# Feed-forward products of two float16 parts in place of two float32r parts, in a kernel of recurrent attention and a max-out feed-forward

## The chip, the cores and the metric

The kernel runs on one core of a Trainium2 chip. The metric is the device time of one launch in microseconds (us), the lower the better. A core has a matrix engine (TensorE: PE for its matmuls, PEld for its weight loads), a vector engine (VectorE, DVE), a scalar engine (ScalarE, ACT), GpSimd (POOL), and SyncE (SP), which here only issues DMAs. Each engine has its own list of instructions; they wait for one another through semaphores.

## The reference

```
for t in range(S):                                   # attention: B=4, H=8, S=768, D=48
    cur = einsum('bhd,bhe->bhde', u * k[t], v[t])
    y[t] = einsum('bhd,bhde->bhe', r[t], state + cur)
    state = w * state + einsum('bhd,bhe->bhde', k[t], v[t])
x = y reshaped to (3072 tokens, 384)
h = maximum(maximum(x @ w1, x @ w2), x @ w3)         # w1, w2, w3: 384 x 768
out = h @ w_out                                      # w_out: 768 x 384
```

The feed-forward weights arrive as 64-bit floats, everything else as float32.

## The kernel before

**Stages.** The 768 steps are cut into 12 chunks of 64. Within a chunk the recurrence is written as matmuls: `scores` (24 per half of the heads, r against k), `keys` (24, k against v, which gives the new state) and `values` (48, which gives the attention output), for each of two halves q of the heads. These matmuls read float16 pairs: each number is a high part plus a low part, and a product is three matmuls (high by high, high by low, low by high; `three`, L407). Their weights are 128x128 and 64 or 48 columns move through. The block-shaped weights (`kb`, `ktb`, `vb`, `sb`) are spread from dense tiles by DMAs that SP issues (`spread`, L318); each is a single buffer.

**Feed-forward.** Of each chunk (256 tokens) `x_high` and `x_low` (L463, L467) take the attention output from PSUM into two parts, xh on ACT and xl on DVE. For each of six blocks f of 128 hidden columns and each of the three weights i, `up` (L498) makes nine matmuls of 128x128 by 256 columns into one PSUM bank: three blocks j of the inner dimension, times three products of parts. `first` (ACT, L505) copies the result of i = 0 to m, `least` (DVE, L510) takes the maximum with i = 1 and 2, `h_high` (ACT) and `h_low` (DVE, or POOL for f below 5 from chunk 1 on) split m into parts hh and hl. `down` (L532) makes 54 matmuls a chunk for the output, `leaving` (ACT) copies them out, and ACT issues their DMAs. So a chunk has 162 + 54 = 216 feed-forward matmuls, 2592 in all. All of their operands are of type float32r (F32R): a float32 whose high part keeps 12 bits, and a low part. A matmul of this type is one instruction of the program, which loads its weights itself. PSUM has four banks for these results (`psm`), each used again when DVE or ACT has read it.

**Weights.** In the first 75 us the eight weight tiles, each as two halves, are loaded and turned from 64-bit floats into parts: `tops` (ACT), `convert` (DVE), `round_up` (ACT, the high part), `leave` (DVE, the low part). The conversion holds for ordinary numbers only, so at the end the kernel loads all weights again (`again`, L706: a DMA of 576 KB, `vet_words` on DVE and `vet_sum` on ACT for each half) and counts exponents out of bounds. `check` (DVE, L562) joins this with sums of squares of r, k, v and the state (`square_sum`, ACT), a matmul of one column (`count`) adds up over partitions, and `verdict` sets a flag. Where the flag is set, `general` (L584) computes everything anew; it does not run with these inputs.

**Order.** Each piece of work is noted by `do` (L65) with an engine, a due time in chunks, a cost and what it reads and writes. `Plan.order` (L84) plays them through as a list scheduler: at each step it takes the ready piece that can start first, and among those close together the one with the earliest due time, shifted by kind through a table (`SHIFT`, L46). The order of the play is the program's order on each engine. A changed cost or an added piece can thus move any piece behind it. For chunks up to 2 DVE does the work that POOL does later (`helper`, L360).

Of the kernel before, what the change touches and what calls it, by code (L numbers as in the profile page):

```python
# [26 lines left out]
U = 8  # L27
# [7 lines left out]
SC_X = 2.0 ** -23  # L35
# [115 lines left out]
def kernel(ctx, tc, feat, tok, wu, ut, ws, wo, cst, out):  # L151
# [102 lines left out]
    beyond = const.tile([P, 1], F32, name="beyond")  # L254
    nc.gpsimd.memset(beyond, -14.5 * 2 ** 23)

    def uppers(raw):
        return raw.bitcast(I32)[:, 0:2 * HN].rearrange("p (n two) -> p n two", two=2)[:, :, 1]

    def vet_words(raw):  # L260
        t = uppers(raw)
        nc.vector.tensor_scalar(out=t, in0=t, scalar1=0x3F800000, scalar2=0x7F800000, op0=ALU.bitwise_xor, op1=ALU.bitwise_and)

    def vet_sum(k, raw):
        t = uppers(raw)
# [78 lines left out]
    stat = const.tile([P, 4, 2 * NCH], F32, name="stat")  # L344
    nc.vector.memset(stat[:, 3], 0.0)

    def square_sum(src, kind, c, q, scale=1.0):
        junk = tmp.tile([P, U, D], BF16, name="junk", bufs=1)
        nc.scalar.activation(out=junk, in_=src, func=AF.Square, scale=scale, accum_out=stat[:, kind, 2 * c + q:2 * c + q + 1])  # L349
# [117 lines left out]
    def x_low(c, q, xh, xl):  # L467
        ps = raws[c, q].pop("va")
        for (hi, src), (lo, _) in zip(x_parts(xh, q, ps), x_parts(xl, q, ps)):
            nc.vector.scalar_tensor_tensor(out=lo, in0=src, scalar=SC_X, in1=hi.bitcast(F32), op0=ALU.mult, op1=ALU.subtract)  # L470

# [25 lines left out]

    def up(x, f, i, n):  # L498
        ps = psm.tile([P, n], F32, name="psm")
        prods = [(wup[:, f, i, j, :], t[:, j, :]) for j in range(NJ) for t in x]  # L500
        prods += [(by_up(lows[f], i, j), x[0][:, j, :]) for j in range(NJ)]
        pairs3(ps, prods)
        return ps

    def first(ps, n):  # L505
        m = tmp.tile([P, n], F32, name="m", bufs=3)
        nc.scalar.copy(out=m, in_=ps)  # L507
        return m

    def least(ps, m, to):  # L510
        nc.vector.tensor_tensor(out=to, in0=ps, in1=m, op=ALU.max)  # L511
# [7 lines left out]
    def h_low(c, h, f, m):  # L519
        lows_by(c, f).tensor_tensor(out=h[1][:, f, :], in0=m, in1=h[0][:, f, :].bitcast(F32), op=ALU.subtract)  # L520

    def up_all(x, h, f, n):
        for i in range(3):
            ps = up(x, f, i, n)
            if i == 0:
                m = first(ps, n)
            else:
                least(ps, m, m)
        h_high(h, f, m)
        h_low(0, h, f, m)  # L530
# [31 lines left out]
    def check():  # L562
        ok = small.tile([P, 8 * NCH + 1 + 2 * NF + 4], F32, name="ok")
# [5 lines left out]
        nc.vector.tensor_scalar(out=ok[:, 8 * NCH + 1:], in0=odd, scalar1=0.0, scalar2=None, op0=ALU.is_equal)  # L569
        got["good"] = small.tile([P, 1], F32, name="good")  # L570
        nc.vector.tensor_reduce(out=got["good"], in_=ok, axis=AX.X, op=ALU.min)
# [12 lines left out]
    def general():  # L584
        def convert_any(n, h):
            hi, lo = part_of(n, h)
# [16 lines left out]
            nc.vector.tensor_tensor(out=t, in0=t, in1=m, op=ALU.bitwise_or)  # L603
            t = t.bitcast(F32)
            nc.scalar.copy(out=hi, in_=t)
            nc.vector.tensor_tensor(out=lo, in0=t, in1=hi.bitcast(F32), op=ALU.subtract)
# [38 lines left out]
        with tc.For_i(0, NCH // 2, 1) as i:  # L645
            for b in range(B):
# [14 lines left out]
                x = xtile(P)  # L661
                nc.scalar.copy(out=x[0], in_=ps)
                nc.vector.tensor_tensor(out=x[1], in0=ps, in1=x[0].bitcast(F32), op=ALU.subtract)
                h = [hp.tile([P, NF, P], F32R, name=f"h{s}") for s in "hl"]
                for f in range(NF):
                    up_all(x, h, f, P)
# [145 lines left out]
    def leave_x(c, q, due):  # L812
        def x_hi():
            if q == 0:
                T["x", c] = [xp.tile([P, NJ, TOK], F32R, name="xh"), None]
            x_high(c, q, T["x", c][0])

        def x_lo():
            if q == 0:
                T["x", c][1] = xp.tile([P, NJ, TOK], F32R, name="xl")  # L820
# [23 lines left out]
    def ffn(c):  # L844
        x = [("xh", c), ("xl", c)]
        for f in range(NF):
            due = c + 0.11 * f
            for i in range(3):
# [3 lines left out]
                do(due + 0.035 * i, "pe", 1.075, mul, reads=[*x, *["stirred"] * (not c and not f), *((a, f, h) for a in ("his", "lo") for h in parts[i])], takes=[("psm", ("up", c, f, i))])  # L852
                if i == 0:
                    do(due - 0.2, "act", act(TOK), lambda f=f: do_tile(("m", c, f), first(T["up", c, f, 0], TOK)), reads=[("up", c, f, 0)], writes=[] if f else [("begun", c)], takes=[("m", ("m", c, f))])
                    continue
                do(due + 0.035 * i - 0.2, "dve", dve(TOK), lambda f=f, i=i: least(T["up", c, f, i], T["m", c, f], T["m", c, f]), reads=[("up", c, f, i)], writes=[("m", c, f)])

            def hi(f=f):
                if f == 0:
                    T["h", c] = [hp.tile([P, NF, TOK], F32R, name="hh")]  # L860
                h_high(T["h", c], f, T["m", c, f])

            def lo(f=f):
# [49 lines left out]
    do(NCH - 0.4, "dve", 1.5, check, reads=["ends", "odd", *(k for k in plan.wrote if k[0] == "sq")], writes=["good"])  # L913
# [67 lines left out]
```

## Time and profile before

| | |
|---|---|
| three runs | 417.0, 418.95 and 419.32 us, median 418.95 |
| the profiled execution | span of 415.5 us from first to last instruction; its launch is not timed apart, and the runs are 1.5 to 3.8 us longer than this span |
| PE, PEld | 394.2 us (95%), 388.5 us (94%), 4768 matmuls |
| DVE | 284.0 us (68%) |
| ACT | 257.7 us (62%) |
| POOL | 183.5 us (44%) |
| DMA | 90.13 MB, mean 217 GB/s |

Matmuls are pipelined: one of 256 columns is recorded as some 285 ns long though the next starts about 118 ns after it. What a matmul costs is therefore read from the distance between starts, or from a stretch of many divided by their count.

### The profile page before, as it was taken

What the parts mean: (1) busy time and instruction counts of PE and PEld (TensorE: products, weight loads), DVE (VectorE), ACT (ScalarE), POOL (GpSimd) and SP (SyncE); (2) the same over time, 40 slices, a digit from 0 to 9 for tenths busy, and PEclk for the clock granted to TensorE, in tenths of its full rate; (3) what the DMA queues carried; (4) which work ended last, traced back from release to release, by engine and by line L of the source; (5) the groups of instructions that cost most, each with busy time, mean ns of one, the idle gap of its engine ahead of it and who ended that gap; (6) DMA issues with size and microseconds to landing.
All of it is one profiled execution on the core that took longest, in us unless ns stands there. A gap on an engine that the chain in (4) does not pass through costs nothing.

```text
span 415.5 us, 11992 instructions
## 1 busy us (share of the span) xinstructions
PE 394.2 (95%) x4768; PEld 388.5 (94%) x4768; DVE 284.0 (68%) x551; ACT 257.7 (62%) x674; POOL 183.5 (44%) x181
## 2 busy tenths in 40 slices
PE   2889899989999999999999999999999999999995
PEld 2768899989999999999999999999999999999994
DVE  6888999988697676767566567566667596353340
ACT  5999987885766556465456466465465476365331
POOL 9000000287668663764664764764664560020120
PEclk9996999999999999999999999999999999999999
DMA  7898998889899887795785785785785996886001
GB/s 280 319 321 210 268 298 273 230 230 265 210 280 243 241 225 189 224 238 142 227 222 152 231 235 144 227 228 150 229 231 130 321 290 147 262 288 206 24 3 44
DMA packets 30959, 90.13 MB, mean 217 GB/s; under 512 B 4784, under 2 KB 9648, under 8 KB 30896
## 3 DMA queue, kind: packets, MB, share of 16 engines
q1 hardware_dynamic: 25568, 84.47, 71.2%
q10 hardware_dynamic: 5328, 4.82, 3.7%
q8 instruction: 39, 0.64, 0.7%
q14 instruction: 24, 0.20, 0.2%
HBM read 45.85 MB, written 4.72 MB: 122 GB/s over the span
## 4 chain that ended last, share of the span: by engine, by line
PE 72%; ACT 9%; DMA 7%; DVE 7%; issue 2%; POOL 1%; SPq 0%; ACTq 0%; DVEq 0%; POOLq 0%
PE psm L496 61%; PE psa L409 11%; ACT junk L349 2%; DMA ktb<-ktd 2%; DMA kb<-kd 2%; ACT ztop L239 2%; DMA out_dram<-io 1%; DVE m L511 1%; DVE wl L250 1%; ACT xh L465 1%; ACT wh L246 1%; DMA sb<-sd 1%; DVE feat L366 1%; ACT kb L476 1%; DVE kd L337 1%
## 5 line engine op out<-in xcount | busy, mean ns | idle before, releaser
L496 PE MATMUL psm<-xh,wh 128*128 128x256 f32 x648 | 165.8, 286 | 2.1 <-ACT m L507 1.3
L496 PE MATMUL psm<-xl,wh 128*128 128x256 f32 x648 | 163.1, 282 | 1.3 <-DVE xl L470 1.3
L496 PEld LDWEIGHTS psm<-xh,wh 128*128 128x128 f32 x648 | 122.9, 190 | 3.0 <-ACT m L507 1.5
L496 PEld LDWEIGHTS psm<-xl,wh 128*128 128x128 f32 x648 | 122.5, 189 | 1.8 <-DVE xl L470 1.8
L496 PE MATMUL psm<-xh,wl 128*128 128x256 f32 x648 | 112.5, 283 | 0.0
L511 DVE TENSOR_TENSOR m<-psm,m 128x256 f32<-128x256 f32 x144 | 60.4, 420 | 67.4 <-PE psm L496 59.3
L496 PEld LDWEIGHTS psm<-xh,wl 128*128 128x128 f32 x648 | 92.6, 189 | 0.0
L366 POOL TENSOR_TENSOR feat<-feat,wrt 128x512 f32<-128x512 f32 x36 | 47.5, 1332 | 76.8 <-DVE sd L339 69.1
L520 POOL TENSOR_TENSOR hl<-m,hh 128x256 fp32r<-128x256 f32 x55 | 45.8, 835 | 68.6 <-ACT hh L514 68.6
L514 ACT CAST hh<-m 128x256 fp32r<-128x256 f32 x72 | 28.9, 405 | 58.0 <-DVE m L511 57.6
L496 PE MATMUL psm<-hh,woh 128*128 128x256 f32 x216 | 54.3, 284 | 0.0
L496 PE MATMUL psm<-hh,wl 128*128 128x256 f32 x216 | 53.4, 279 | 0.0
L385 POOL TENSOR_TENSOR am<-tok,u_sb 128x384 f32<-128x384 f32 x18 | 20.7, 1151 | 61.3 <-DVE al L429 61.3
L349 ACT ACTIVATE junk<-tok 128x384 bf16<-128x384 f32 x72 | 37.4, 520 | 9.2 <-DMA tok<-in_tok_dram 7.6
L496 PEld LDWEIGHTS psm<-hh,woh 128*128 128x128 f32 x216 | 40.6, 188 | 0.0
L496 PEld LDWEIGHTS psm<-hh,wl 128*128 128x128 f32 x216 | 40.6, 188 | 0.0
L470 DVE SCALAR_TENSOR_TENSOR xl<-psa,xh 32x256 fp32r<-32x256 f32 (+2 forms) x60 | 28.3, 472 | 14.1 <-ACT xh L465 13.2
L465 ACT ACTIVATE xh<-psa 32x256 fp32r<-32x256 f32 (+2 forms) x60 | 25.1, 418 | 17.1 <-PE psa L409 16.2
L496 PE MATMUL psm<-hl,woh 128*128 128x256 f32 x216 | 35.1, 280 | 0.0
L409 PE MATMUL psa<-ah,vb 128*128 128x64 f16 x352 | 32.8, 194 | 1.4 <-ACT junk L349 1.4
L507 ACT COPY m<-psm 128x256 f32<-128x256 f32 x72 | 26.4, 368 | 10.0 <-PE psm L496 8.7
L409 PE MATMUL psa<-rh,sb 128*128 128x64 f16 x352 | 32.5, 193 | 0.0
(102 smaller groups left out, 741.4 us busy)
## 6 DMA issues: line engine op xcount, KB each, us to landing
tok<-in_tok_dram SPq DMA_DIRECT2D x24, 576.0 KB, 6.6
raw<-in_ws_dram SPq DMA_DIRECT2D x24, 576.0 KB, 7.7
feat<-in_feat_dram SPq DMA_DIRECT2D x24, 512.0 KB, 5.4
kb<-kd SPq DMA_DIRECT2D x22, 256.0 KB, 5.1
kb<-kd SPq DMA_DIRECT2D x22, 248.0 KB, 5.6
ktb<-ktd SPq DMA_DIRECT2D x20, 256.0 KB, 3.5
ktb<-ktd SPq DMA_DIRECT2D x20, 248.0 KB, 4.1
raw<-in_wo_dram SPq DMA_DIRECT2D x8, 576.0 KB, 5.6
```

Source lines behind the costliest of these rows:

```text
L239: nc.scalar.copy(out=ztop[h].bitcast(F16).rearrange("p (n two) -> p n two", two=2)[:, :, 1], in_=halves(raw[:, 1:], 3).bitcast(BF16))
L349: nc.scalar.activation(out=junk, in_=src, func=AF.Square, scale=scale, accum_out=stat[:, kind, 2 * c + q:2 * c + q + 1])
L366: helper(c).tensor_tensor(out=t[n], in0=t[n], in1=tb, op=ALU.mult)
L385: helper(c).tensor_tensor(out=w.rearrange("p (g b) d -> p g b d", g=2), in0=t["r"], in1=by_token(u_sb, q), op=ALU.mult)
L409: nc.tensor.matmul(out=ps, lhsT=l[i], rhs=rr[j], start=first and n == 0, stop=last and n == 2)
L465: nc.scalar.mul(out=hi, in_=src, mul=SC_X)
L470: nc.vector.scalar_tensor_tensor(out=lo, in0=src, scalar=SC_X, in1=hi.bitcast(F32), op0=ALU.mult, op1=ALU.subtract)
L496: nc.tensor.matmul(out=ps, lhsT=a, rhs=b, start=first and n == 0, stop=last and n == len(prods) - 1)
L507: nc.scalar.copy(out=m, in_=ps)
L511: nc.vector.tensor_tensor(out=to, in0=ps, in1=m, op=ALU.max)
L514: nc.scalar.copy(out=h[0][:, f, :], in_=m)
L520: lows_by(c, f).tensor_tensor(out=h[1][:, f, :], in0=m, in1=h[0][:, f, :].bitcast(F32), op=ALU.subtract)
```

## The change

All feed-forward operands become pairs of float16 in place of pairs of float32r: weights (one tile per weight block that holds both parts, `wsp`), xh and xl, hh and hl. Powers of two keep them in the range of the type (`X16`, `W16`, `H16`), so copies out of PSUM become multiplications: `first` and `leaving` on ACT, and `least` on DVE, which becomes a scalar_tensor_tensor in place of a tensor_tensor. `leave`, too, becomes a scalar_tensor_tensor. A float16 matmul of the program is two instructions, a weight load and a matmul.

The second load of the weights goes, with `vet_words` and `vet_sum`; in place of them ACT squares and sums the high part of each half weight (`weight_sum`, 16 times 576 columns) and of each chunk's x (`x_sum`, 12 times 768 columns), and `check` compares those sums with bounds: 17 instructions in place of 12. The planner's costs of `up` and `down` are lowered. `general` computes in plain float32.

```diff
-SC_X = 2.0 ** -23
+X16, W16, H16 = 2.0 ** 13, 2.0 ** 14, 2.0 ** -20
+SC_X = X16 * 2.0 ** -23
+SC_O = 1.0 / (X16 * W16 * W16 * H16)
...
-    wup = const.tile([P, NF, 3, NJ, P], F32R, name="wh")
-    wdn = const.tile([P, NF, DM], F32R, name="woh")
-    odd = const.tile([P, 2 * NF + 4], F32, name="odd")
+    wsp = [const.tile([P, 2, WN], F16, name=f"w{n}") for n in range(NW)]
+    wsq = const.tile([P, 2 * NW], F32, name="wsq")
...
-    lows = [const.tile([P, WN], F32R, name=f"wl{n}") for n in range(NW)]
...
     def round_up(n, h, raw):
-        nc.scalar.copy(out=part_of(n, h)[0], in_=mids(raw).bitcast(F32))
+        nc.scalar.mul(out=part_of(n, h)[0], in_=mids(raw).bitcast(F32), mul=W16)
 
     def leave(n, h, raw):
         hi, lo = part_of(n, h)
-        nc.vector.tensor_tensor(out=lo, in0=mids(raw).bitcast(F32), in1=hi.bitcast(F32), op=ALU.subtract)
...
+        nc.vector.scalar_tensor_tensor(out=lo, in0=mids(raw).bitcast(F32), scalar=W16, in1=hi, op0=ALU.mult, op1=ALU.subtract)
+
+    def squared(src, to):
+        junk = tmp.tile([P, NJ * TOK], BF16, name="junk", bufs=1)
+        nc.scalar.activation(out=junk[:, 0:src.shape[1]], in_=src, func=AF.Square, accum_out=to)
+
+    def weight_sum(n, h):
+        squared(part_of(n, h)[0], wsq[:, 2 * n + h:2 * n + h + 1])
...
+    def x_sum(c, xh):
+        squared(xh.rearrange("p j n -> p (j n)"), xsq[:, c:c + 1])
...
-    def first(ps, n):
+    def first(ps, n, by):
         m = tmp.tile([P, n], F32, name="m", bufs=3)
-        nc.scalar.copy(out=m, in_=ps)
+        nc.scalar.mul(out=m, in_=ps, mul=by)
         return m
 
-    def least(ps, m, to):
-        nc.vector.tensor_tensor(out=to, in0=ps, in1=m, op=ALU.max)
+    def least(ps, m, by):
+        nc.vector.scalar_tensor_tensor(out=m, in0=ps, scalar=by, in1=m, op0=ALU.mult, op1=ALU.max)
...
     def again(n, h, due):
-        w = ("vet", n, h)
-
-        def fetch():
-            T[w] = load_weight(n, h)
-
-        dma(due, fetch, 8 * P * HN, reads=[("begun", int(due))], takes=[("raw64", w)])
-        do(due + 0.4, "dve", 0.4, lambda: vet_words(T[w]), writes=[w])
-        do(due + 0.5, "act", act(HN) + 0.1, lambda: vet_sum(2 * n + h, T[w]), reads=[w], writes=["odd"])
+        do(due + 0.5, "act", act(HN) + 0.1, lambda: weight_sum(n, h), reads=[("his", n, h), ("begun", int(due))], writes=[("wsq", n, h)])
...
+        if q:
+            do(due + 0.9, "act", act(NJ * TOK) + 0.1, lambda: x_sum(c, T["x", c][0]), reads=[hi], writes=[("xsq", c)])
...
-                do(due + 0.035 * i, "pe", 1.075, mul, reads=[*x, *["stirred"] * (not c and not f), *((a, f, h) for a in ("his", "lo") for h in parts[i])], takes=[("psm", ("up", c, f, i))])
+                do(due + 0.035 * i, "pe", 0.983, mul, reads=[*x, *["stirred"] * (not c and not f), *((a, f, h) for a in ("his", "lo") for h in parts[i])], takes=[("psm", ("up", c, f, i))])
...
-            do(due, "pe", len(fs) * 0.358, lambda: down(T["h", c], m, fs, banks, TOK), reads=reads, **(dict(takes=[("psm", bank)]) if 0 in fs else dict(writes=[bank])))
+            do(due, "pe", len(fs) * 0.328, lambda: down(T["h", c], m, fs, banks, TOK), reads=reads, **(dict(takes=[("psm", bank)]) if 0 in fs else dict(writes=[bank])))
```

From chunk 4 on PE keeps its order of stages: in both programs a chunk's round is 99 `up` matmuls, values, keys and scores, 54 `down` matmuls, 45 `up`, values, 9 `up`, keys, 9 `up`, scores. Earlier the order shifts. Three places matter for what follows.

**PE, from chunk 2 to chunk 3.** In the program before, PE's last rows ahead of chunk 3's first `up` (operands xh and xl, weights wh) are the `down` of chunk 2 (hh and hl); values, scores and keys stand ahead of those 54:

```order
L496 MATMUL psm<-hh,woh 128x256
L496 MATMUL psm<-hh,wl_108 128x256
L496 MATMUL psm<-hh,woh 128x256
L496 MATMUL psm<-hh,wl_108 128x256
L496 MATMUL psm<-hl,woh 128x256 x6
L496 MATMUL psm<-xh,wh 128x256
L496 MATMUL psm<-xl,wh 128x256
```

In the changed program (weights w_98 to w_105) the last `down` rows of chunk 2 stand ahead of the 48 values matmuls (vb, sb), which make the second half of chunk 3's x:

```order
L487 LDWEIGHTS w_105
L487 MATMUL psm<-hl,w_105 128x256
L487 LDWEIGHTS w_105
L487 MATMUL psm<-hl,w_105 128x256
L400 LDWEIGHTS vb_135
L400 MATMUL psa<-ah,vb_135 128x64
```

Behind these 48 come 24 scores and 24 keys matmuls (ktb), and then at once chunk 3's first `up`:

```order
L400 LDWEIGHTS ktb
L400 MATMUL psa<-vd_143,ktb 128x48
L400 LDWEIGHTS ktb
L400 MATMUL psa<-vd_143,ktb 128x48
L487 LDWEIGHTS w_98
L487 MATMUL psm<-xh,w_98 128x256
L487 LDWEIGHTS w_98
L487 MATMUL psm<-xl,w_98 128x256
```

So between the values matmuls and the `up` that reads their result stand 48 matmuls of 64 or 48 columns now, and stood 102 before, 54 of them of 256 columns.

**ACT, at chunk 0's x.** Before, behind the last rows of `x_high` (L465), the first evacuation of an `up` (L507, m from psm) stands behind the work on r, the diagonal (am), the squares and three `round_up` (wh):

```order
L465 ACTIVATE xh<-psa 32x256 x3
L239 CAST ztop_110<-raw_275 128x576
L246 CAST wh<-raw_268 128x576
L371 CAST rh<-feat 128x512
L476 ACTIVATE ktb<-tok 64x8x48 x2
L397 ACTIVATE am<-cs,a 128x64 x8
L239 CAST ztop_109<-raw_295 128x576
L349 ACTIVATE junk,stat<-tok 128x384 x3
```

In the changed program the sum of squares of x (xsq) is put in, and the first evacuation (L502) is the eighth row behind `x_high`:

```order
L456 ACTIVATE xh<-psa 32x256 x3
L237 CAST ztop_108<-raw_272 128x576
L244 ACTIVATE w_100<-raw_265 128x576
L252 ACTIVATE junk,xsq<-xh 128x768
L362 CAST rh<-feat 128x512
L467 ACTIVATE ktb<-tok 64x8x48 x2
L237 CAST ztop_107<-raw_292 128x576
L244 ACTIVATE w_100<-raw_272 128x576
L502 ACTIVATE m<-psm 128x256
```

Before, that evacuation was the row behind the fourth `round_up` that follows `x_high`; two of these `round_up`, the diagonal, the squares and the parts of v, state and k now stand behind it.

**The last chunk.** On ACT of the changed program the last three sums over weights (wsq) stand behind the first evacuation of chunk 11:

```order
L502 ACTIVATE m<-psm 128x256
L252 ACTIVATE junk,wsq<-w_104 128x576
L252 ACTIVATE junk,wsq<-w_105 128x576 x2
L509 CAST hh<-m 128x256
L502 ACTIVATE m<-psm 128x256
```

On DVE `check` reads them (its last rows here), two `least` rows into chunk 11, and ends in the row that writes good:

```order
L541 TENSOR_TENSOR ok<-ok,bt 128x12
L539 TENSOR_SCALAR bt<-wsq 128x16
L540 TENSOR_SCALAR ok<-wsq 128x16
L541 TENSOR_TENSOR ok<-ok,bt 128x16
L559 TENSOR_REDUCE good<-ok 128x1
L506 SCALAR_TENSOR_TENSOR m<-psm,m 128x256 x2
L567 TENSOR_SCALAR flag<-psa 1x1
```

PE's `count`, which reads good, stood behind 126 of chunk 11's 162 `up` matmuls and stands behind 54 of them now.

More of the change, by code (lines that the diff above doesn't have):

```diff
@@ L200, with part_of, exact @@
     NW = NF + 2
+    wsp = [const.tile([P, 2, WN], F16, name=f"w{n}") for n in range(NW)]
+    wsq = const.tile([P, 2 * NW], F32, name="wsq")
+    def part_of(n, h):
+        return [wsp[n][:, s, h * HN:(h + 1) * HN] for s in range(2)]
+    def exact(n):
+        return wsp[n].rearrange("p s n -> p (s n)").bitcast(F32)
     def by_up(t, i, j):
@@ L344 @@
     stat = const.tile([P, 4, 2 * NCH], F32, name="stat")
+    xsq = const.tile([P, NCH], F32, name="xsq")
     nc.vector.memset(stat[:, 3], 0.0)
     def square_sum(src, kind, c, q, scale=1.0):
-        junk = tmp.tile([P, U, D], BF16, name="junk", bufs=1)
-        nc.scalar.activation(out=junk, in_=src, func=AF.Square, scale=scale, accum_out=stat[:, kind, 2 * c + q:2 * c + q + 1])
+        junk = tmp.tile([P, NJ * TOK], BF16, name="junk", bufs=1)
+        nc.scalar.activation(out=junk[:, 0:U * D].rearrange("p (u d) -> p u d", u=U), in_=src, func=AF.Square, scale=scale, accum_out=stat[:, kind, 2 * c + q:2 * c + q + 1])
     def units(a):
@@ L519, in h_low @@
     def h_low(c, h, f, m):
[L520 to L530, printed above, removed]
+        lows_by(c, f).tensor_tensor(out=h[1][:, f, :], in0=m, in1=h[0][:, f, :], op=ALU.subtract)
     def down(h, m, fs, banks, n):
@@ L536, in down, with w, leaving @@
         ms = slice(m * P, (m + 1) * P)
-        prods = [(t, hh[:, f, :]) for f in fs for t in (wdn[:, f, ms], by_down(lows[NF + f // 3], f, ms))]
-        prods += [(wdn[:, f, ms], hl[:, f, :]) for f in fs]
+        def w(f, s):
+            return by_down(wsp[NF + f // 3][:, s], f, ms)
+        prods = [(w(f, s), hh[:, f, :]) for f in fs for s in range(2)]
+        prods += [(w(f, 0), hl[:, f, :]) for f in fs]
         pairs3(banks[m], prods, 0 in fs, NF - 1 in fs)
-    def leaving(ps, n):
+    def leaving(ps, n, by):
         o = tmp.tile([P, n], F32, name="io", bufs=3)
-        nc.scalar.copy(out=o, in_=ps)
+        nc.scalar.mul(out=o, in_=ps, mul=by)
         return o
-    def xtile(n):
-        return [xp.tile([P, NJ, n], F32R, name=f"x{s}") for s in "hl"]
     def bounded(dst, src, lo, hi):
@@ L602, in convert_any @@
             ts(out=m, in0=rw[:, :, 1], scalar1=-2 ** 31, scalar2=None, op0=ALU.bitwise_and)
[L603 to L606, printed above, removed]
+            nc.vector.tensor_tensor(out=exact(n)[:, h * HN:(h + 1) * HN].bitcast(I32), in0=t, in1=m, op=ALU.bitwise_or)
         for n in range(NW):
@@ L660, in general @@
                     nc.tensor.transpose(out=ps[:, j], in_=xt[:, j], identity=ident)
[L661 to L664, printed above, removed]
+                x = xp.tile([P, NJ, P], F32, name="xh")
+                nc.scalar.copy(out=x, in_=ps)
+                h = hp.tile([P, NF, P], F32, name="hh")
                 for f in range(NF):
-                    up_all(x, h, f, P)
+                    for e in range(3):
+                        ps = psm.tile([P, P], F32, name="psm")
+                        pairs3(ps, [(by_up(exact(f), e, j), x[:, j, :]) for j in range(NJ)])
+                        if e == 0:
+                            nc.scalar.copy(out=h[:, f, :], in_=ps)
+                        else:
+                            nc.vector.tensor_tensor(out=h[:, f, :], in0=ps, in1=h[:, f, :], op=ALU.max)
                 def put(m, o):
@@ L669, in put @@
                     nc.sync.dma_start(out=ov, in_=o.rearrange("p (i two s) -> p i two s", i=1, two=2))
-                banks = {}
                 for m in range(NM):
-                    down(h, m, range(NF), banks, P)
-                    put(m, leaving(banks[m], P))
+                    ps = psm.tile([P, P], F32, name="psm")
+                    pairs3(ps, [(by_down(exact(NF + f // 3), f, slice(m * P, (m + 1) * P)), h[:, f, :]) for f in range(NF)])
+                    put(m, leaving(ps, P, 1.0))
     plan = Plan(dict(feat=2, tok=3, raw64=4, psa=4, psm=4, rh=2, rl=2, am=2, a=2, ah=1, al=1, xh=2, xl=2, m=3, io=3, hh=1, hl=1))
@@ L819, in x_lo @@
             if q == 0:
-                T["x", c][1] = xp.tile([P, NJ, TOK], F32R, name="xl")
+                T["x", c][1] = xp.tile([P, NJ, TOK], F16, name="xl")
             x_low(c, q, *T["x", c])
@@ L912 @@
     do(4.9, "dve", 1.2, check_ends, reads=[("begun", 4)], writes=["ends"])
-    do(NCH - 0.4, "dve", 1.5, check, reads=["ends", "odd", *(k for k in plan.wrote if k[0] == "sq")], writes=["good"])
+    do(NCH - 0.4, "dve", 1.5, check, reads=["ends", *(k for k in plan.wrote if k[0] in ("sq", "xsq", "wsq"))], writes=["good"])
     do(NCH - 0.35, "pe", 0.1, count, reads=["good"], takes=[("psa", "count")])
```

41 lines of the change are left out of this document (13 added, 28 removed).

## The prediction

> **What bounds the kernel now.** I read first the busy times by stretch of the span, to see where one engine is full. A row has the stretch, its length, the busy time of each engine (with instructions), the granted clock of TensorE, the share of the DMA engines and their GB/s. Two more stretches, which serve further down, are added.
>
> ```profile
> PE 394.2 (95%) x4768; PEld 388.5 (94%) x4768; DVE 284.0 (68%) x551; ACT 257.7 (62%) x674; POOL 183.5 (44%) x181
> ...
> 36.00:38.80 2.80, 2.80 (x14) 2.80 (x14) 2.42 (x6) 2.71 (x8) 0.00 (x0) 0.50 0.76 182
> 39.40:40.40 1.00, 1.00 (x10) 1.00 (x10) 0.64 (x1) 1.00 (x4) 0.00 (x0) 1.00 0.85 186
> 40.00:75.00 35.00, 33.66 (x428) 33.31 (x427) 33.77 (x68) 29.96 (x69) 0.00 (x0) 1.00 0.88 264
> 75.00:102.00 27.00, 24.80 (x334) 24.39 (x334) 23.35 (x38) 20.44 (x62) 19.06 (x16) 1.00 0.92 257
> 102.00:137.00 35.00, 33.80 (x463) 33.20 (x462) 27.76 (x49) 23.51 (x65) 24.68 (x22) 1.00 0.89 233
> 137.00:410.40 273.40, 273.40 (x3410) 271.73 (x3408) 166.47 (x335) 149.84 (x399) 129.19 (x124) 1.00 0.70 198
> ```
>
> From 137 us, where chunk 3's feed-forward begins, to 410.4 us PE is never idle, while DVE works 61% of the time, ACT 55%, POOL 47% and the DMA engines 70%. There the kernel is PE's work and nothing else. From 40 to 75 us DVE is as full as PE (33.77 of 35 us), since it converts the weights and does POOL's work; that stage has two bounds. Next, how many feed-forward matmuls (one line, L496) lie in each stage:
>
> ```profile
> 42.70:136.70 94.00, 75.60 (x612) 73.04 (x613) 1.00 0.90 253
> 136.70:410.40 273.70, 236.75 (x1946) 231.00 (x1945) 1.00 0.70 198
> ```
>
> So 612 in the two-bound stage and 9 chunks of 216 = 1944 in the PE-bound one (the row has two that straddle its edge). What one costs comes from the chain of work that ended last, in order of time (start, length, line, count); here one whole round of a chunk:
>
> ```profile
> 255.33 11.73 PE psm L496 x99
> 267.06 1.42 PE psa L409 x48
> 268.47 1.14 PE psm L496 x9
> 269.61 0.61 PE psa L409 x24
> 270.23 1.15 PE psm L496 x9
> 271.37 0.72 PE psa L409 x24
> 272.09 11.75 PE psm L496 x99
> 283.84 2.72 PE psa L409 x96
> ```
>
> The 216 feed-forward matmuls take 11.73 + 1.14 + 1.15 + 11.75 = 25.77 us, **119.3 ns each**; the float16 attention matmuls take 5.47 us, and the round 31.2 us.
>
> **The matmuls, the main term.** The trace has float16 matmuls of 64 columns, with a weight load of 128x128 each, and a few of 256 columns in the opening (`stir`):
>
> ```profile
> 26.12 2.34 PE L492 MATMUL psm<-still 128*128 128x256 f16 x10
> 36.47 0.41 PE L496 MATMUL psm<-xh,wh 128*128 128x256 f32 x1
> 36.68 0.41 PE L496 MATMUL psm<-xl,wh 128*128 128x256 f32 x1
> 39.46 0.28 PE L496 MATMUL psm<-xh,wh 128*128 128x256 f32 x1
> 39.58 0.28 PE L496 MATMUL psm<-xl,wh 128*128 128x256 f32 x1
> L492 PE MATMUL psm<-still 128*128 128x256 f16 x10 | 2.3, 421 | 0.0
> L409 PEld LDWEIGHTS <-vb 128*128 128x128 f16 x528 | 27.3, 98 | 3.4 <-DMA vb<-vd 1.5 <-issue 0.9
> ```
>
> The ten of `stir` stand (2.34 - 0.42) / 9 = 0.213 us apart. Float32r matmuls stand as far apart (36.47, 36.68) in the stretch whose granted clock is 0.50. At that pace the type makes no difference, which is the row against this change. At clock 1.00 (39.46, 39.58) float32r stands 0.12 apart; half of 0.213 would be 0.1065, so some 12 ns each are an extra that did not halve. Whether float16 has that extra, too, no row of 256 columns shows. The nearest is the 48 of 64 columns in 1.42 us: 29.6 ns each, against a quarter of 106.5, 26.6. Their extra is 3.0 ns. The bounds are thus 106.5 ns (none) and 118.4 (29.6 times four, no gain). I take the fixed extra of the nearest row: 106.5 + 3.0 = 109.5, and for transitions between groups 0.3 more: **109.8**, a saving of 9.5 ns. In the PE-bound stage that is 1944 x 9.5 = **18.5 us** (bounds 1.7 and 24.9).
>
> A rule of the Trainium skill speaks against it ("TensorE: Matmul & The Clock Gate", Part 3): a weight load overlaps matmuls in flight only when it is for another row group. Here all loads fill all rows, so each would be paid, and the sum would be some 229 us slower in place of 18.5 faster. The trace differs: its 29.6 ns are shorter than the weight load of 98 ns among them, so loads do overlap. The third rival below is this mechanism, worked out from rows.
>
> Will the others keep up with a round of 29.2 us in place of 31.2? Work for 31.2 us is, by the last stretch, 19.0 us on DVE, 17.1 on ACT, 14.7 on POOL. Changed instructions there: `least` becomes a scalar_tensor_tensor reading PSUM; the closest form, `x_low`, takes no longer:
>
> ```profile
> L511 DVE TENSOR_TENSOR m<-psm,m 128x256 f32<-128x256 f32 x144 | 60.4, 420 | 67.4 <-PE psm L496 59.3 <-ACT m L507 6.1 <-ACT hh L514 0.5
> L470 DVE SCALAR_TENSOR_TENSOR xl<-psa,xh 96x256 fp32r<-96x256 f32 x12 | 5.0, 413 | 3.5 <-ACT xh L465 3.5
> L520 POOL TENSOR_TENSOR hl<-m,hh 128x256 fp32r<-128x256 f32 x55 | 45.8, 835 | 68.6 <-ACT hh L514 68.6
> L349 ACT ACTIVATE junk<-tok 128x384 bf16<-128x384 f32 x72 | 37.4, 520 | 9.2 <-DMA tok<-in_tok_dram 7.6
> L349 ACT ACTIVATION_READ_ACCUMULATOR junk<-tok 128x1 f32 x72 | 13.5, 188 | 0.0
> L507 ACT COPY m<-psm 128x256 f32<-128x256 f32 x72 | 26.4, 368 | 10.0 <-PE psm L496 8.7 <-POOL tok L405 0.5 <-POOL hl L520 0.2
> ```
>
> `x_sum` is a Square of 768 columns. From 256 to 384 columns ACT's rows rise by 520 - 368 = 152 ns, so 768 take about 520 + 3 x 152 = 976 ns, and the accumulator's 188: at most 1.16 us a chunk, hidden behind ACT's idle 14 us a round. POOL has no row with float16: its five `h_low` a chunk take 835 ns; at half that or at double (4.2 us more) POOL has room. `leave` and `round_up` pass the same 576 columns each as before. I count these edits at nothing; cover gone, they would cost their sums, 1.2 and 4.2 us a round. The second load of the weights, its DMAs and its work on DVE and ACT, lies after 333 us beside a full PE: nothing to gain.
>
> **The stage up to 137 us.** PE's 612 matmuls shrink by 5.8 us. Three things take from it. (1) DVE: 33.77 of 35 us busy, with the same instructions to do; ACT even gets `x_sum` three times, 3.5 us at most. (2) The new order at chunk 3: the `up` now comes right behind 24 scores and 24 keys (0.72 + 0.61 = 1.33 us by the round above), and it must wait for x. What that takes is seen at the same place of a round:
>
> ```profile
> 254.06 1.56 ACT L465 ACTIVATE xh<-psa 96x256 fp32r<-96x256 f32 x4 [0.49 <-PE psa L409]
> 256.00 1.74 DVE L470 SCALAR_TENSOR_TENSOR xl<-psa,xh 96x256 fp32r<-96x256 f32 x4
> ```
>
> The values matmuls end at about 253.9, xl at 257.74: 3.8 us, of which 1.33 are covered, so PE stalls some **2.5 us** once. Before, 54 `down` covered it. (3) Chunk 2 stands similarly, with less cover than before: some 1 us. Bounds of the stage: a gain of 5.8 (all of it, stalls absorbed where PE waits today) and a loss of 2 (DVE and ACT set the pace, and the stalls come on top). 5.8 - 2.5 - 1.3 = **2.0 us**, with 0.3 of the 1.3 for ACT.
>
> **The last chunk.** `count` stands behind 54 `up` now, 54 x 109.8 = 5.9 us into the chunk, and PE waits there for good; all of PE's later matmuls are queued behind it. ACT's first evacuation ends about 1.6 us in, three sums over weights follow (576 columns, by the rise above 0.75 + 0.19 us each), to 4.4 us; two `least` end by 3.6 us, and `check` reads the statistics first. `check` in the trace:
>
> ```profile
> 396.80 0.18 DVE L552 TENSOR_SCALAR bt<-stat 128x48 f32<-128x48 f32 x1
> ...
> 398.52 0.27 DVE L571 TENSOR_REDUCE good<-ok 128x1 f32<-128x113 f32 x1
> ```
>
> 12 instructions in 1.99 us, so 17 take about 2.8: good is there 6.4 us in, and PE waits **0.5 us** (0 to 1.2). The kernel's end moves by as much, since PE's later work has no cover.
>
> **The sum.** 415.5 - 18.5 - 2.0 + 0.5 = 395.5 us for the span. The median of the runs lies 418.95 - 415.5 = 3.45 us above the profiled span, and the end (a copy of 0.37 us and a DMA) stays as it is: **399 us**.
>
> **Rivals.** *The opening eats more*: DVE and ACT keep their pace to 137 us, the stalls add 2 us to it: 415.5 - 18.5 + 2 + 0.5 + 3.45 = 403. For it speaks DVE's 33.77 of 35; against it, that DVE has 3.65 us idle from 75 to 102. *Everything is gained*: 5.8 in the opening and no wait for good: 394.6; for it, PE's idle times there (1.34 and 2.2 us in the two rows) may serve as cover. *The weight loads come out*: a float16 pair is two instructions, and beside 256 columns a load might not hide as it does beside 64. Its place is every one of the 2592 pairs, its full price 98 - 9.5 = 88.5 ns a pair, 229 us, and a time of 648; it decides from 9.5 exposed ns of 98 on, where the change turns slower. At 20 exposed ns it is 418.95 + 2592 x 10.5 ns = 446. Against it stands the 29.6 ns row. *The type makes no difference at full clock either* (118.4 ns): 415.5 - 1.7 + 0.5 + 3.45 = 418, the change does not do what it says; for it, the equal 0.213 us at half clock.
>
> **How the numbers follow.** Forecast 58%, the opening eats more 19%, everything gained 16%, no difference 4%, loads come out 3%. Within the forecast the saving may be 7.5 to 11.5 ns a matmul, 14.6 to 22.4 us, so 395 to 403; the rivals beside it reach to 392 and 406 with the same spread. The range is 392 to 406. About 0.5%, 2.1 us, is what a measurement of this kernel can tell from no change. Faster than that: forecast, the two neighbours, 93% and 1% of "no difference"; same 3%; slower 3%.
>
> **What would show it.** In the changed profile: float16 `up` matmuls 109 to 110 ns apart and a round of 29.1 us; PE full from chunk 3 to the end; chunk 3's first `up` at 132 to 137 us, with a PE wait for `x_low` of 2 to 3 us just ahead; a PE wait of about 0.5 us at `count`. Wrong would be: PE idle in the rounds, released by DVE, ACT or a DMA; a distance of 118; weight loads that stand between matmuls.

## The result, and the profile after

The changed kernel takes 404.7 us (median of four runs, 403.35 to 407.54) beside 417.98 us for the kernel before on the same occasion: a ratio of 0.970, 95% interval 0.965 to 0.975. It is faster by 3%. The forecast was 399 us, so 5.7 us of the expected gain did not arrive, though the range held the time. The profiled execution took 405.38 us, with a span of 403.5 us where the sum had 395.5. The times given below for the experiments are medians that leave out runs over 1.5% above the fastest run of the same kernel.

First the busy times of the whole span, then by stretch (length, busy time and instructions of PE, PEld, DVE, ACT, POOL, granted clock, DMA share, GB/s):

```profile
PE 372.7 (92%) x4768; PEld 334.0 (83%) x4768; DVE 276.7 (69%) x540; ACT 265.1 (66%) x698; POOL 182.2 (45%) x180
...
40.00:75.00 35.00, 30.32 (x378) 26.33 (x376) 31.98 (x64) 29.11 (x68) 0.00 (x0) 0.95 0.81 223
75.00:102.00 27.00, 24.97 (x347) 22.08 (x346) 18.46 (x35) 20.42 (x65) 16.21 (x16) 1.00 0.94 266
102.00:137.00 35.00, 31.42 (x456) 27.80 (x456) 26.42 (x49) 22.90 (x63) 19.46 (x19) 1.00 0.86 219
137.00:146.00 9.00, 8.34 (x64) 6.17 (x64) 7.16 (x11) 5.79 (x18) 7.16 (x6) 0.63 1.04 273
146.00:398.40 252.40, 249.39 (x3352) 226.59 (x3347) 159.99 (x320) 152.86 (x409) 128.85 (x122) 1.00 0.64 172
```

PE has become less full up to 137 us (30.32 of 35 in place of 33.66, 31.42 of 35 in place of 33.80), while no other engine has become full: what it saved there it spends waiting. From 137 to 146 us the granted clock is 0.63, where it was 1.00 before. From 146 us on PE is 99% busy, but not all. One round of that last stretch, from the chain of work that ended last (start, length, line, count):

```profile
253.35 10.81 PE psm L487 x99
264.16 1.40 PE psa L400 x48
265.56 0.98 PE psm L487 x9
266.55 0.60 PE psa L400 x24
267.14 0.98 PE psm L487 x9
268.13 0.70 PE psa L400 x24
268.83 10.81 PE psm L487 x99
279.63 2.70 PE psa L400 x96
```

The 216 feed-forward matmuls take 10.81 + 0.98 + 0.98 + 10.81 = 23.58 us, 109.2 ns each in place of 119.3: 10.1 ns saved, and the round takes 29.0 us (29.1 forecast). The changed instructions, by line (count, busy, mean ns, idle before):

```profile
L487 PEld LDWEIGHTS <-w 128*128 128x128 f16 x2592 | 252.2, 99 | 45.3 <-issue 14.4
L515 POOL TENSOR_TENSOR hl<-m,hh 128x256 f16<-128x256 f32 x55 | 45.6, 830 | 148.5 <-ACT hh L509 74.6
L506 DVE SCALAR_TENSOR_TENSOR m<-psm,m 128x256 f32<-128x256 f32 x144 | 60.1, 419 | 63.8 <-PE psm L487 37.5
L502 ACT ACTIVATE m<-psm 128x256 f32<-128x256 f32 x72 | 27.1, 378 | 14.2 <-PE psm L487 10.5
```

A weight load of 99 ns lies wholly beside a matmul that starts every 109 ns. `h_low` takes 830 ns (835 before), `least` 419 (420), `first` 378 (368): counted at nothing, rightly.

At chunk 3's first `up`, by the timeline (start, length, what, in brackets the idle time before and its end):

```profile
134.32 0.76 PE L400 MATMUL psa<-vd,ktb 128*128 128x48 f16 x24 [0.29 <-DMA ktb<-ktd]
135.65 0.27 PE L487 MATMUL psm<-xh,w 128*128 128x256 f16 x1 [0.57 <-ACT xh L456]
137.66 0.37 PE L487 MATMUL psm<-xl,w 128*128 128x256 f16 x1 [1.74 <-DVE xl L461]
...
141.50 0.42 PE L487 MATMUL psm<-xl,w 128*128 128x256 f16 x1
141.72 0.42 PE L487 MATMUL psm<-xh,w 128*128 128x256 f16 x1
...
143.79 0.27 PE L487 MATMUL psm<-xl,w 128*128 128x256 f16 x1
143.90 0.27 PE L487 MATMUL psm<-xh,w 128*128 128x256 f16 x1
```

The wait for x is there as forecast, 0.57 + 1.74 us. What was not forecast comes behind it: starts 0.21 us apart on average until 143.7 us, then 0.11. The record of the granted clock is 0.5 from 136.9 to 143.73 us. From 137.66 us on the other 44 of these 45 `up` took 7.8 us; at 109.2 ns each they take 4.8.

**A common scale.** Executions of one kernel differ in their first 29 us (by 2.5 us in two of the profiles below), so places are counted from the first matmul of `stir`. As marks serve the starts of the second half's `values` of chunks 2, 3 and 4 ("values 2" to "values 4" in the table) and the first `down` matmul of the last chunk ("last `down`"). For chunk 4, in the changed kernel:

```profile
26.11 2.03 PE L483 MATMUL psm<-still 128*128 128x256 f16 x10
...
160.91 0.19 PE L400 MATMUL psa<-ah,vb 128*128 128x64 f16 x1
```

and in the kernel before, whose `stir` began at 26.12:

```profile
158.76 0.20 PE L409 MATMUL psa<-ah,vb 128*128 128x64 f16 x1
```

That is 134.8 us after `stir` in place of 132.6: so far the change has lost 2.2 us. From there to the last `down` 245.2 us became 231.5, a gain of 13.7. All profiles by this scale (us from the first `stir`), with the ratio to the kernel before on the same chip, which is taken from the runs other than the profiled one:

| kernel | values 2 | values 3 | values 4 | last `down` | ratio (95%) |
|---|---|---|---|---|---|
| before | 69.1 | 100.9 | 132.6 | 377.8 | 1 |
| changed | 70.1 | 105.7 | 134.8 | 366.3 | 0.970 (0.965 to 0.975) |
| changed, second time (E9) | 68.8 | 104.6 | 132.7 | 365.7 | 0.970 (0.966 to 0.973) |
| E1 float16, order of before | 71.5 | 101.8 | 136.0 | 367.9 | 0.976 (0.966 to 0.985) |
| E2 float32r, order of the change | 69.3 | 105.5 | 133.5 | 379.3 | 1.011 (1.006 to 1.017) |
| E3 no sums of x | 69.9 | 105.2 | 134.4 | 368.1 | 0.969 (0.963 to 0.974) |
| E4 late `count` | 70.9 | 107.5 | 137.0 | 366.8 | 0.973 (0.967 to 0.978) |
| E5 filled wait | 70.7 | 107.3 | 134.0 | 367.8 | 0.973 (0.969 to 0.977) |
| E6 half of feat | 70.0 | 104.1 | 133.7 | 364.4 | 0.966 (0.961 to 0.970) |
| E7 no squares | 68.4 | 104.3 | 132.7 | 364.0 | 0.966 (0.962 to 0.970) |
| E8 float32r, half of feat | 69.5 | 100.5 | 131.6 | 376.8 | 0.995 (0.991 to 0.998) |
| E10 filled wait, late `count` | 70.0 | 105.1 | 132.8 | 363.3 | 0.969 (0.964 to 0.973) |
| E11 no low halves of weights | 67.8 | 102.4 | 130.4 | 360.3 | 0.969 (0.964 to 0.973) |
| E12 short `up` in chunks 0 to 2 | 71.7 | 106.3 | 135.5 | 367.7 | 0.973 (0.969 to 0.977) |

The two executions of the changed kernel lie 2.1 us apart at chunk 4: a smaller difference of single marks says nothing. By E9 the change has lost only 0.1 us up to chunk 4, and gains 12.2 us from there.

### The profile page after: what moved, and what is told of

Its sections match the earlier page's. It is cut to its first block, busy times and chain, and to the rows that moved or that the text cites. A ratio compares the mean times of both kernels' runs of the same rounds, so it can differ in the third digit from the quotient of the medians.

```text
span 403.5 us, 11979 instructions
## 1 busy us (share of the span) xinstructions
PE 372.7 (92%) x4768; PEld 334.0 (83%) x4768; DVE 276.7 (69%) x540; ACT 265.1 (66%) x698; POOL 182.2 (45%) x180
## 4 chain that ended last, share of the span: by engine, by line
PE 43%; DMA 16%; ACT 8%; DVE 6%; issue 3%; ACTq 1%; SPq 1%; POOL 0%; DVEq 0%
PE psm L487 36%; PE psa L400 7%; DMA kb<-kd 6%; DMA tok<-in_tok_dram 4%; DMA feat<-in_feat_dram 3%; DMA ktb<-ktd 3%; ACT xh L456 2%; ACT junk L340 1%; ACTq L867 1%; ACT junk L252 1%; DVE m L506 1%; DVE ktd L327 1%; ACT kd L322 1%; ACT rh L362 1%; ACT io L532 1%
## 5 line engine op out<-in xcount | busy, mean ns | idle before, releaser
L487 PEld LDWEIGHTS <-w 128*128 128x128 f16 x2592 | 252.2, 99 | 45.3 <-issue 14.4
L487 PE MATMUL psm<-xh,w 128*128 128x256 f16 x1296 | 226.3, 276 | 5.4 <-ACT m L502 2.7
L487 PE MATMUL psm<-xl,w 128*128 128x256 f16 x648 | 156.1, 276 | 5.3 <-DVE xl L461 4.9
L515 POOL TENSOR_TENSOR hl<-m,hh 128x256 f16<-128x256 f32 x55 | 45.6, 830 | 148.5 <-ACT hh L509 74.6
L506 DVE SCALAR_TENSOR_TENSOR m<-psm,m 128x256 f32<-128x256 f32 x144 | 60.1, 419 | 63.8 <-PE psm L487 37.5
L487 PE MATMUL psm<-hh,w 128*128 128x256 f16 x432 | 55.7, 273 | 0.0
L502 ACT ACTIVATE m<-psm 128x256 f32<-128x256 f32 x72 | 27.1, 378 | 14.2 <-PE psm L487 10.5
L487 PE MATMUL psm<-hl,w 128*128 128x256 f16 x216 | 33.5, 273 | 0.7 <-POOL hl L515 0.7
L400 PE MATMUL psa<-al,vb 128*128 128x64 f16 x176 | 31.7, 195 | 0.6 <-DVE al L420 0.6
L400 PE MATMUL psa<-rl,sb 128*128 128x64 f16 x176 | 31.7, 195 | 0.0
L400 PEld LDWEIGHTS <-vb 128*128 128x128 f16 x528 | 29.8, 100 | 1.4 <-issue 0.8
```

The costliest lines, as they stand in the source:

```text
L400: nc.tensor.matmul(out=ps, lhsT=l[i], rhs=rr[j], start=first and n == 0, stop=last and n == 2)
L487: nc.tensor.matmul(out=ps, lhsT=a, rhs=b, start=first and n == 0, stop=last and n == len(prods) - 1)
L502: nc.scalar.mul(out=m, in_=ps, mul=by)
L506: nc.vector.scalar_tensor_tensor(out=m, in0=ps, scalar=by, in1=m, op0=ALU.mult, op1=ALU.max)
```

## The experiments

The theories: T1, the new order of the opening and the clock that drops behind its stall gave the gain back; T2, up to chunk 4 the attention's chain sets the pace, whatever PE does; T3, a DMA in the rounds (the spread of `kb`), or ACT's added squares, cost the time; T4, the DMA engines as a whole set the pace of the opening.

### E1 and E2: order and arithmetic apart

E1 takes the change back to the planner's costs of before:

```diff
-do(due + 0.9, "act", act(NJ * TOK) + 0.1, lambda: x_sum(c, T["x", c][0]), ...
+do(due + 0.9, "act", 0.0, lambda: x_sum(c, T["x", c][0]), ...
-do(due + 0.035 * i, "pe", 0.983, mul, ...
+do(due + 0.035 * i, "pe", 1.075, mul, ...
-do(due, "pe", len(fs) * 0.328, lambda: down(...
+do(due, "pe", len(fs) * 0.358, lambda: down(...
```

> The change with the planner's two costs of a feed-forward group put back to 1.075 and 0.358, and the sum of squares of x planned at no cost, so that PE's order up to chunk 3 is that of the kernel before; the arithmetic stays in float16. T1 (the new order of the opening gives the gain there back: the stalls at chunk 2 and chunk 3, and a clock that drops to 0.5 behind the stall): chunk 3's first up starts at 133 to 135 us in place of 137.7, no half clock behind it, time 398 to 400. T2 (DVE, ACT and the attention's chain set the opening, whatever the order): the start stays at 136 to 138, time 403 to 405. T3 (a DMA in the rounds, kb in scores of chunk 4 and after, costs the time): 403 to 405 as well, with kb waits as in the changed kernel.

E2 puts the change's costs, and a place for `x_sum` that issues nothing, into the kernel before.

> The kernel before (float32r) with the planner's costs of the change and a planned place for a sum of squares of x that issues nothing, so that PE's order up to chunk 3 is that of the change. T1 (order alone costs): the stall of about 2 us at chunk 3 shows here too, and the kernel is 2 to 5 us slower than before, 420 to 423 us. T2 (order is not what matters): 417 to 419. T3: no change, 417 to 419.

Measured: E1 407.0 us (ratio 0.976) with chunk 3's first `up` at 140.2 us, both beyond what any of the theories expected; E2 421.0 us (ratio 1.011), as T1 had it. The marks say more than the times. Chunk 3's values begin at 100.9 and 101.8 us in the old order, at 105.5 and 105.7 in the new one (104.6 in E9): the order moves them by 3 to 5 us, and the arithmetic by no more than the spread. By chunk 4 the old order has lost its lead with float16, and all but 0.9 us of it with float32r. With float32r the new order costs 0.6 to 1.7%; with float16 going back to the old one brings nothing that shows, though E1's interval is wide. E1 contradicts T1's order as an account of the whole shortfall. It does not test T1's clock: in E1, too, the granted clock was 0.5 for 3.41 us behind a wait of 1.8 us for `ktb`, from 132.0 us on. Why the old order brings nothing is seen in the chain of work that ended last; E1's row (start, length) ahead of chunk 3's `keys`, and behind it the same row of the kernel before:

```profile
122.28 9.77 DMA ktb<-ktd
132.05 0.14 issue
132.18 1.13 PE psa L400 x24
```

```profile
120.53 9.06 DMA ktb<-ktd
129.59 0.14 issue
129.73 0.76 PE psa L409 x24
```

PE waits for the spread of `ktb` in both (1.8 us in E1, 0.4 us before), and a faster PE comes there no sooner. The 24 `keys` behind it take 1.13 us at the lower clock, 0.76 us at the full one.

### E3: the squares of x

```diff
-do(due + 0.9, "act", act(NJ * TOK) + 0.1, lambda: x_sum(c, T["x", c][0]), ...
+do(due + 0.9, "act", act(NJ * TOK) + 0.1, lambda: None, ...
```

> The change without the sums of squares of x: nothing is issued on ACT at their places, and the statistics that they feed are filled with a constant; the order is unchanged. If ACT's added work in the opening holds x back (T3, second part): chunk 3's first up 1 to 2 us sooner and 401 to 403 us. T1 and T2: the squares lie beside other work, 404 to 405.5.

Measured: 403.84 us, ratio 0.969, marks as in the change. The squares cost nothing that shows; the time lies just below T1's and T2's 404 to 405.5 us, above T3's 401 to 403.

### E4: the wait at count

```diff
-"pe count": (0, -1.9)
+"pe count": (0, 0.0)
```

> The change with the last chunk's count behind all 162 up of that chunk in place of 54. If PE's wait at count of about 1.1 us in the changed kernel's trace is on the path (all theories): 0.9 us less, 403.5 to 404, with no wait for good. If what follows count (the sums and the end) needs it early: no change or up to 1 us more.

The changed kernel's row of waits (engine line waited for: us, times, longest):

```profile
PE psa L563 <- DVE good L559: 0.9, 1, 0.9
```

Measured: the row is gone. From the last chunk's second `values` to the last `down` E4 takes 25.20 us, the change 26.15 (26.15 in E9, too; 25.20 in E10): 0.95 us saved at its place. The time, 405.2 us in place of the expected 403.5 to 404, does not show it: the interval of its ratio (0.967 to 0.978) is some 5 us wide, and the opening of the profiled execution was 2 us longer (137.0 at chunk 4).

### E5 and E10: filling the wait ahead of chunk 3

```diff
+        if fill:
+            pairs3(ps, [(by_up(wh, 0, 0), wsp[1][:, 0, 0:n])] * fill)
         pairs3(ps, prods)
...
-up(T["x", c], f, i, TOK)
+up(T["x", c], f, i, TOK, 18 if (c, f, i) == (3, 0, 0) else 0)
```

> The change with 18 further matmuls of 256 columns (weights by weights, into the bank that the first up then starts anew) put ahead of chunk 3's first up, where PE waits some 2 us for x in the changed kernel. They take 18 x 109 ns = 2.0 us beside that wait; the result is unchanged. T1, clock part (the wait is what drops the granted clock to 0.5 behind it, from 136.9 to 143.7 us): no half clock between 130 and 150 us, chunk 3's values at 142 to 143 us in place of 145.4, time 401 to 403. Rival (the clock drops for another cause, such as the load of all engines there): the half clock stays, and 404 to 406.

E10 has this and E4's edit.

> The change with the 18 further matmuls in the wait ahead of chunk 3's first up, and count behind all 162 up of the last chunk. The local savings seen in the two single runs were 2.9 us (no half clock behind chunk 3's wait) and 1.1 us (no wait for good). If they add up to the end: 4 us less than the changed kernel on the same chip, 400 to 401.5. If what is saved at chunk 3 is lost to waits for kb and x in chunks 4 and 5 (T2, the attention sets the pace there too): 1 to 2 us less, 402.5 to 404.

E9 is the changed kernel again, on E10's chip.

> The changed kernel as it is, on the chip of the next three, as their base. All theories: 404 to 405.5 us, ratio to the kernel before 0.966 to 0.972; chunk 4's values (second half) begin 134 to 137 us behind the first matmul of stir, as in the runs so far with this order.

Stretches of E9 (length, PE busy, granted clock, DMA share, GB/s):

```profile
134.00:136.00 2.00, 0.27 (x1) 0.94 1.01 337
136.00:140.00 4.00, 3.68 (x21) 0.60 1.03 294
140.00:144.00 4.00, 4.00 (x74) 1.00 1.03 253
```

and of E10:

```profile
134.00:136.00 2.00, 2.00 (x79) 1.00 0.95 298
136.00:140.00 4.00, 3.85 (x39) 1.00 1.05 347
140.00:144.00 4.00, 4.00 (x54) 1.00 1.03 268
```

The eight profiles of float16 kernels in this order without the filling (changed, E3, E4, E6, E7, E9, E11, E12) all have a half clock that begins between 135.5 and 140.9 us; the two with it have none. So at this place the wait causes the drop; the load of the DMA engines is as high in E10. There the drop cost 3.0 us in the change and 1.4 in E9 (44 `up` in 7.8 and 6.2 us against 4.8). But E10's runs (403.6 us, ratio 0.969) can't be told from E9's (404.9 us, ratio 0.970), and its values of chunk 4 begin where E9's do: in E10's profile PE had already waited 1.94 us for `sb` in chunk 3's values, ahead of the filling. E9's own mark at chunk 4, 132.7 us, lies below the 134 to 137 expected. E5 came out in the clock as T1 said; its time, 408.6 us on a chip where the kernel before took 419.3, lies above the ranges of T1 and of the rival. What the clock costs locally is shown; that taking the drop away shortens the run is not.

### E6, E7, E8, E11: less work for DMA, ACT and DVE

E6 and E8 load half of `feat` in chunks 1 to 4, in the changed kernel and in the kernel before:

```diff
-nc.sync.dma_start(out=f, in_=feat[c, q])
+if 1 <= c <= 4:
+    nc.sync.dma_start(out=f[:, 0], in_=feat[c, q][:, 0])
+else:
+    nc.sync.dma_start(out=f, in_=feat[c, q])
```

> The change without half of the bytes of feat for chunks 1 to 4 (left out: r by columns, which is a tile of zeros there): 8 loads of 256 KB in place of 512 KB, 2.1 MB or some 8 us of the DMA engines' work by their 250 to 270 GB/s, all engines' instructions and PE's order unchanged. T4 (the opening up to chunk 4 is bound by the DMA engines, which stood at 0.81 to 1.04 there): chunk 3's first up starts at 133 to 136 us in place of 137.7, ktb and kb land sooner, fewer PE waits for kb, 398 to 402. T2 (the chain of ACT and DVE work of the attention): 136.5 to 138.5, 403.5 to 405.5.

> The kernel before (float32r) with the same half of feat left out in chunks 1 to 4. If the transfers bind only the faster PE (T4): 415 to 418, as before. If they set the opening of the kernel before as well: chunk 3's first up at 133 to 135 us in place of 136.8 and 412 to 415. T2 with engines as the link: 416 to 418.

E7 leaves out ACT's squares of r, k and v in chunks 1 to 4.

> The change without ACT's sums of squares of r, k and v in chunks 1 to 4 (left out: 24 of the statistics, filled with a constant): 24 x 0.71 us = 17 us less on ACT, and no square that waits for tok ahead of x_high; the rest and PE's order unchanged. T2 with ACT as the link (its in-order work holds x, kd and ktd back): chunk 3's first up at 133 to 136 us, 399 to 402. T4 (DMA): 136.5 to 138.5, 403.5 to 405.5.

E11 leaves out `leave`, the low halves of the weights, on DVE.

> The change without the low halves of the weights (left out: 16 scalar_tensor_tensor of 576 columns on DVE, some 0.67 us each, 10.7 us; the halves are zeros): the order and PE's work are unchanged. T2 with DVE as the link (the conversion of the weights holds chunk 1's and chunk 2's attention back): chunk 2's values begin 64 to 68 us behind the first stir in place of 70.1, chunk 4's 128 to 132 in place of 134.8; 398 to 402. If ACT and the loads set it: chunk 2's values at 69 to 71, 403.5 to 405.5.

Measured: E6 404.1, E8 416.7, E7 404.9 and E11 402.6 us. E8 gained 0.5% on the kernel before (0.2 to 0.9), E6 and E7 0.4% on the change, with intervals that overlap its own. Some 8 us of transfers, 17 us of ACT or 10.7 us of DVE less move chunk 4's values to 133.7, 132.7 and 130.4 us, against 132.7 and 134.8 in the kernel itself. With less transfer or less ACT work alone the time did not come down to what was expected of the link (398 to 402 and 399 to 402 us): T4, and T2 with ACT as its only link, fall as sole causes. The squares of T3 fell with E3; its `kb` takes some 1.4 us in the rounds, as is shown below.

DVE stays open. E11's marks at chunks 2 and 4, 67.8 and 130.4 us, lie in the ranges given for DVE as the link (64 to 68 and 128 to 132), and its chunk 3 (102.4) comes ahead of all others in this order (104.1 to 107.5). But its time lies between the range for DVE (398 to 402) and the other (403.5 to 405.5), its ratio, 0.969, can't be told from E9's, and the profiled execution was the fastest of its six (399.6 us). So DVE's conversions may hold the opening back by some 2 us; that is not shown.

### E12: less work for PE

```diff
-        prods += [(by_up(wl, i, j), x[0][:, j, :]) for j in range(NJ)]
+        if not short:
+            prods += [(by_up(wl, i, j), x[0][:, j, :]) for j in range(NJ)]
...
-up(T["x", c], f, i, TOK)
+up(T["x", c], f, i, TOK, c < 3)
```

> The change with the products of the weights' low halves left out of up in chunks 0 to 2: 162 matmuls less, 162 x 109 ns = 17.7 us less work on PE up to chunk 3; all else and the order as in the change. T2 (up to chunk 4 the attention's chain sets the pace, and PE's work is not what counts): chunk 4's values begin 132 to 136 us behind the first stir, and 402 to 405. If PE's work sets the opening: 117 to 122, and 387 to 390. In between: the share of the 17.7 us that arrives tells how much of the opening is PE's.

Measured: 406.1 us, ratio 0.973; chunk 4's values at 135.5 us. The mark lies in T2's range; the time lies 1 us above T2's 402 to 405, and 16 us above the 387 to 390 expected if PE's work set the opening. Of 17.7 us less work on PE nothing arrived. E9's stretches (columns as in the first table of stretches):

```profile
40.00:75.00 35.00, 32.19 (x426) 28.15 (x425) 32.74 (x66) 30.17 (x72) 0.00 (x0) 1.00 0.83 233
75.00:102.00 27.00, 24.94 (x349) 22.25 (x346) 19.71 (x39) 20.21 (x65) 17.06 (x16) 1.00 0.97 261
102.00:137.00 35.00, 30.90 (x452) 27.43 (x453) 26.69 (x47) 23.50 (x64) 19.21 (x19) 0.98 0.85 223
```

and E12's, with its waits from 40 to 137 us behind them:

```profile
40.00:75.00 35.00, 28.39 (x349) 23.04 (x348) 33.26 (x67) 30.45 (x73) 0.00 (x0) 0.88 0.87 242
75.00:102.00 27.00, 21.93 (x294) 18.93 (x292) 18.82 (x34) 19.74 (x61) 15.31 (x15) 0.94 0.92 242
102.00:137.00 35.00, 27.77 (x426) 23.77 (x422) 23.69 (x44) 21.34 (x59) 18.90 (x20) 0.95 0.80 206
...
PE psa L400 <- DMA kb<-kd: 5.2, 2, 4.0
PE psm L487 <- DVE m L507: 3.7, 2, 2.2
PE psa L400 <- DMA ktb<-ktd: 3.3, 3, 2.7
```

PE is idle 18.9 us of these 97 in place of 9.0, and its busy time fell by only 9.9 us, because behind the idle stretches the clock came down to 0.88 to 0.95 on average, which is worth 35 x 0.12 + 27 x 0.06 + 35 x 0.05 = 7.6 us of full clock. So what E12 shows is that some 10 us less of PE's busy time move nothing: the opening does not go faster with PE, as T2 has it. That the whole 17.7 us would move nothing at full clock is not shown.

## Why the prediction was right, and what of it was not

**The matmuls: right, and a little small.** 109.8 ns were forecast, 109.2 measured; the saving is 10.1 ns in place of 9.5. At half clock the starts are 0.213 us apart, at full clock 109.2 ns, so 2.7 ns did not halve, as the 64-column row had it (3.0). The rivals "weight loads come out" and "the type makes no difference" are out. With them falls, for these shapes, the rule of the Trainium skill ("TensorE: Matmul & The Clock Gate", Part 3) as it was weighed there: loads of 99 ns lie beside matmuls that start 109.2 ns apart.

**The rounds: fewer of them at full pace than assumed.** From chunk 4's values to the last `down` lie 1728 feed-forward matmuls: 16.4 us by the forecast, 17.5 by the measured 10.1 ns, 13.7 arrived. What is missing is PE's waits: 0.95 us at `count`, 1.39 us for `kb` in chunk 5's scores (starts 192.33 and 193.72 us), and smaller ones for `least` and `first`. PE is idle for 3.0 of these 231.5 us (4.2 of 233.0 in E9), where before it was idle for none. That PE stays full from chunk 3 to the end was wrong by about 1%, and PE idle in the rounds, released by DVE, ACT or a DMA, was one of the forecast's own signs of being wrong. The transfer at that place took:

```profile
184.79 8.88 DMA kb<-kd
```

The other engines are now close behind PE: in the first profile its part of the chain of work that ended last fell from 72% to 43%, and that chain passes through transfers of `kb` in the rounds at 184, 214 and 301 us.

**The stage up to 137 us, the step that failed.** "5.8 - 2.5 - 1.3 = 2.0" held that PE's shorter work arrives and that stalls are subtracted from it. E12 speaks against that: with 162 matmuls less the stage is as long. The rival "the opening eats more" named the right thing and priced it closer, at 403, though for it DVE was to be the pace, and E11 gives DVE some 2 us beside E9, which its runs don't show. The stall at chunk 3 was sized well (2.5 forecast, 0.57 + 1.74 measured), but it is not a term beside the saving: E1, whose order has no stall for x there, comes to chunk 4 no sooner. And this stall cost more than its length: the 3.0 us (1.4 in E9) that the half clock behind it took were in no term. Together, to chunk 4's values, a gain of 2.0 + 162 x 9.5 ns = 3.5 us was forecast, and 2.2 us were lost in the first profile, 0.1 us in E9: the step was 3.6 to 5.7 us too high.

**The last chunk.** 0.5 us forecast (0 to 1.2), 0.95 measured.

**ACT, POOL, the weights.** `x_sum` at nothing: E3 agrees. `h_low` in float16 takes what it took. The second load of the weights, costed at nothing, was not undone alone; that it lay beside a full PE is seen in the kernel before, whose rounds last 31.2 us both ahead of it and beside it.

**The sum.** The span came out 403.5 where 395.5 was forecast, 8.0 us longer: some 5.7 to chunk 4's values and 2.2 behind them (3.6 and 3.7 in E9). In the time 5.7 us of it are left, by luck. The distance of 3.45 us from span to time was a term too large: in the runs with both numbers it is 1.7 to 2.5 us (1.9 in the profiled run, 405.38 against 403.5), so the profiled execution of before was shorter than the median, which hid 1.6 us. The profiled run after lies 0.7 us above its median.

**What stays open.** Which link of the attention's chain sets the opening. Taking 8 us of transfers, 17 of ACT or 10.7 of DVE away one at a time moved the mark at chunk 4 by 2.3 us at most beyond E9's, and the spread of two executions is 2.1 us. The chain of work that ended last goes there through transfers of `tok`, `ktb` and `kb` that each take 5 to 11 us, with ACT and DVE work between, so several links in a row would fit; taking two of them away together was not tried. No variant that computes everything was shown faster than the change: the best, E10, had 403.6 us beside 404.9 for E9, with ratios of 0.969 and 0.970.

## What to carry to other kernels

What an instruction saves counts only in the stretch where its engine sets the pace, and PE at 92 to 97% busy in the opening before was not yet proof of that; leaving out 162 of the 648 feed-forward matmuls of chunks 0 to 2 (E12), once they are float16, made the stage no shorter. A gain in a stage that other engines feed is best sized at nothing until that is tried. And a planner whose costs are changed moves the waits: the two orders here differ by 3 to 5 us at one mark and have lost that lead 30 us later.

## What the runs showed of the hardware

In these profiles the granted clock halved behind rather short waits. In the fourteen profiles PE was idle for 1.74 us or more 18 times between 40 and 392 us, and 17 times a stretch of granted clock 0.5, of 3.41 or 6.83 us, began in the wait or within 6 us behind it (the exception is E10's 1.94 us for `sb`); of five waits of 1.5 to 1.7 us one had it, and once, in E12 at 55.4 us, it came behind two waits of 1.17 and 0.68 us within 2.1 us. The Trainium skill ("TensorE: Matmul & The Clock Gate", "Why this matters for your kernels") advises against idle gaps of over about 3 us; here little more than half of that was enough. At full clock a float32r matmul of 256 columns takes 12.8 ns more than half of its 213 ns at half clock (119.3 against 106.5, over a whole round), a float16 one with its own weight load 2.7 (109.2 against 106.5).
